# All four weight pairs of the first half issued by ScalarE

## The chip, the cores and the metric

The kernel runs on one core of one Trainium2 chip. The metric is the device time of one execution, in microseconds. Of the 40 runs of the kernel before, 39 lie within 0.2% of their median of 486.8 us (all from 486.38 to 488.38), and the effect told here is only a few times that, so kernels are compared by several runs taken in alternation with the kernel before on the same chip. A "ratio" in this document is the mean time of one kernel's fast runs over the mean of the other's fast runs of the same rounds, so it is not quite the ratio of the medians that stand beside it.

## The reference

Two attention blocks share an input x of 2048 rows by 1024 columns (bf16): block A is linear attention, block B a dilated sliding window. A gate mixes their outputs. The first thing that either needs is x times a weight matrix; the kernel begins with block B's v.

```python
qkv = x @ wqkv            # x: 2048 x 1024, wqkv: 1024 x 3072, for block A and for block B
...                       # attention of each block, then @ wo
g = sigmoid((x * gate_w).sum(-1, keepdims=True))
return g * a + (1 - g) * b
```

## The kernel before

The kernel is a list of operations with dependencies and priorities, which a small scheduler of its own puts in order for each engine before the program is built. Only the head of the program matters here. The x tile of rows 128t to 128t+127 is loaded by a DMA transpose and called x0, x1, ... below. The weights of v come in two halves of 512 columns; each half is loaded as four "pairs", each of two 128-row chunks, 256 KB.

```python
def load_x(t, prio):
    e_, r = t // 8, t % 8
    return P.op("sp", lambda e: e.dma_start_transpose(xT[:, :, t * 128:(t + 1) * 128], x2[e_, r * 128:(r + 1) * 128, :]),
                1.5, writes=[xT.part((0, 8), (t * 128, (t + 1) * 128))], prio=prio, chan="x%d" % t, lat=1.3)

def load_w(slot, half, src, c0, prio, d0=0, d1=8, eng="sp", after=()):
    n = d1 - d0
    return P.op(eng, lambda e: e.dma_start(ws[slot][:, d0:d1, half * 512:half * 512 + 512], src[:, d0:d1, c0:c0 + 512]), ...)

load_x(0, 0)                                       # x0, SyncE
load_w(0, 0, Bw, 2048, 0.1, 0, 2, "act")           # half one, pair 1, ScalarE
load_w(0, 0, Bw, 2048, 0.2, 2, 4, "act")           # pair 2, ScalarE
load_w(0, 0, Bw, 2048, 0.3, 4, 6)                  # pair 3, SyncE
load_w(0, 0, Bw, 2048, 0.4, 6, 8)                  # pair 4, SyncE
for t in range(1, NT):
    load_x(t, 3 + t)                               # x1 ... x15, SyncE
for d in range(0, 8, 2):
    load_w(0, 1, Bw, 2560, 6.1 + 0.1 * d, d, d + 2)   # half two, four pairs, SyncE
# ... cut: warm-up matmuls on a zeroed tile ...
for t, half in [(4 * b + i, half) for b in range(NT // 4) for half in range(2) for i in range(4)]:
    # ... cut ...
    step = 2 if t == 0 else 8
    for d in range(0, 8, step):                    # x0: two matmuls as each pair lands; others: eight at once
        o = group(bank, xs, w, [xr, ws[0].part((d, d + step), (half * 512, half * 512 + 512))], d, d + step)
    # ... cut: eviction to vst by ScalarE or VectorE, then a store by SyncE ...
```

The matmul engine thus runs x0 with pairs 1 to 4 (eight matmuls, two for each pair), then x1, x2, x3 with half one (24), then x0 to x3 with half two, and so on.

## Time and profile before

| | before |
|---|---|
| time, median of the first 3 runs | 486.82 us (486.45 to 486.95) |
| profiled span | 485.2 us |
| matmul engine busy | 474.2 us, 98% |
| first real matmul | 5.54 us |
| matmuls without another wait for a load from | 15.30 us |

From the page of the kernel before: the span, the busy line (PE is the matmul engine, PEld its weight loads, then VectorE, ScalarE, GpSimd; x counts instructions), and the first line of the chain that ended last.

```profile
span 485.2 us, 10105 instructions
...
PE 474.2 (98%) x4339; PEld 222.8 (46%) x4403; DVE 285.2 (59%) x547; ACT 140.2 (29%) x227; POOL 5.9 (1%) x36
...
PE 95%; SPq 2%; issue 1%; DMA 1%; ACT 0%; DVE 0%
```

The matmul engine, busy for 98% of the span and with 95% of the chain that ended last, is the limit almost from end to end. What is left to win is where it waits. The timeline of the head shows that. Columns are start and duration in us, engine (SPq and ACTq are SyncE's and ScalarE's issue of DMAs), line, operation, count, and in brackets the idle time before the piece and what ended it.

```profile
0.80 1.38 SPq L1308 DMA_TRANSPOSE xT<-in_A_x_dram  x1
0.80 0.94 ACTq L1313 DMA_DIRECT2D w<-in_B_wqkv_dram  x2
...
2.24 1.06 SPq L1313 DMA_DIRECT2D w<-in_B_wqkv_dram  x2
...
3.35 4.92 SPq L1308 DMA_TRANSPOSE xT<-in_A_x_dram  x3
...
5.54 1.47 PE L1334 MATMUL ps_all<-w,xT 128*128 128x512 bf16 x6 [0.28 <-DMA xT<-in_A_x_dram]
...
7.25 0.60 PE L1334 MATMUL ps_all<-w,xT 128*128 128x512 bf16 x2 [0.24 <-DMA w<-in_B_wqkv_dram]
...
8.17 6.82 PE L1334 MATMUL ps_all<-w,xT 128*128 128x512 bf16 x30 [0.32 <-DMA xT<-in_A_x_dram]
8.31 2.12 SPq L1313 DMA_DIRECT2D w<-in_B_wqkv_dram  x4
...
15.30 17.00 PE L1334 MATMUL ps_all<-w,xT 128*128 128x512 bf16 x77 [0.30 <-DMA w<-in_B_wqkv_dram]
```

Read it from the fifth line down. The first matmuls start at 5.54, when x0 is there. The last two of x0's eight start at 7.25, when pair 4 is there. The x1 group starts at 8.17, and at 15.30 the last pair of half two ends the last wait. Six, two and thirty matmuls make 38 before 15.30.

The table of stretches of the same kernel gives the DMA rate. The columns used are the stretch, its length, then the busy times, and at the end of the row the granted matmul clock (1.00 is full speed), the DMA share and GB/s. The DMA share is the time that DMA packets took, over sixteen engines; it passes 1 here (1.28 at 6.5 to 7.5 us).

```profile
core 0: us, PE busy (x) PEld busy (x) DVE busy (x) ACT busy (x) POOL busy (x), PEclk, DMA share, GB/s
2.50:5.50 3.00, 2.76 (x9) 0.92 (x7) 1.29 (x10) 0.56 (x1) 2.58 (x14) 1.00 1.08 302
...
6.50:7.50 1.00, 0.76 (x5) 0.13 (x3) 0.19 (x1) 0.00 (x0) 0.00 (x0) 1.00 1.28 267
7.50:8.50 1.00, 0.69 (x4) 0.21 (x3) 0.00 (x0) 0.60 (x1) 0.00 (x0) 1.00 1.14 239
8.50:9.50 1.00, 1.00 (x7) 0.41 (x5) 0.00 (x0) 0.00 (x0) 0.00 (x0) 1.00 1.06 243
9.50:10.50 1.00, 1.00 (x6) 0.47 (x5) 0.00 (x0) 0.39 (x1) 0.00 (x0) 1.00 0.56 110
10.50:11.50 1.00, 1.00 (x7) 0.47 (x5) 0.00 (x0) 0.21 (x1) 0.00 (x0) 1.00 1.06 322
```

A stretch with transposes alone (7.5 to 9.5) moves about 240 GB/s; the stretch from 2.5 to 5.5, for most of which x0 from SyncE ran beside pairs 1 and 2 from ScalarE, moved 302. At 9.5 to 10.5, where SyncE's queue turns from transposes to pairs, there is a slack spot.

One more reading: when each load landed. The trace records sixteen completions for each load. The matmuls that wait for a load start just after its sixteenth (pair 4's at 7.25 us, after 7.21; x1's at 8.17, after 8.13). "Landed" below is the sixteenth, and "spread" is the time from the first to the sixteenth. Before, pair 3 landed at 6.36 us, pair 4 at 7.21 (spread 0.20), x1 at 8.13, x2 at 9.14, x3 at 10.20.

### The profile page before, as it was taken

To read this page: it belongs to the slowest core of one execution; us is meant where nothing else is said; L and a number is where in the kernel's file an instruction comes from. 1 tells how busy PE (TensorE), PEld (TensorE's weight loads), DVE (VectorE), ACT (ScalarE), POOL (GpSimd) and SP (SyncE) were. 2 spreads that over 40 slices of the span, in tenths; PEclk is the share of its full clock that TensorE was granted. 3 is DMA by queue.
4 is the path that set the end of the run, shared out by engine and by line. 5 is a ranking of instruction groups with operands and counts; after the bars stand their busy time and mean duration, and the time that the engine had idled before them with its cause. 6 is when DMAs were issued, how large, how long until landed. Compare 5 with 4: busy or idle time off the path is not lost.

```text
span 485.2 us, 10105 instructions
## 1 busy us (share of the span) xinstructions
PE 474.2 (98%) x4339; PEld 222.8 (46%) x4403; DVE 285.2 (59%) x547; ACT 140.2 (29%) x227; POOL 5.9 (1%) x36
## 2 busy tenths in 40 slices
PE   8999999999999999999999999999999999999997
PEld 3444444444444444454544554444444444444443
DVE  2121435888688888665666556496579236653434
ACT  2111121235322234334443333455532230111000
POOL 4000000000000000000000000000000000000000
PEclk9999999999999999999999999999999999999999
DMA  8999993132014459433222322820086018830212
GB/s 224 222 194 299 309 355 122 65 110 86 1 44 135 107 138 245 100 76 86 55 75 67 85 66 66 204 54 2 10 217 163 1 15 242 221 24 2 88 68 89
DMA packets 72951, 57.39 MB, mean 118 GB/s; under 512 B 37953, under 2 KB 60865, under 8 KB 72898
## 3 DMA queue, kind: packets, MB, share of 16 engines
q1 hardware_dynamic: 72210, 56.07, 44.3%
q8 instruction: 36, 0.59, 0.5%
q10 hardware_dynamic: 688, 0.59, 0.4%
q14 instruction: 17, 0.14, 0.1%
HBM read 34.49 MB, written 13.76 MB: 99 GB/s over the span
## 4 chain that ended last, share of the span: by engine, by line
PE 95%; SPq 2%; issue 1%; DMA 1%; ACT 0%; DVE 0%
PE ps_all L1334 78%; PE ps_all L1693 11%; PE ps_all L1463 2%; PE ps_all L1440 2%; SPq L1308 1%; DMA w<-in_B_wqkv_dram 1%; PE ps_all L1556 1%; SPq L1313 1%; PE ps_all L1638 0%; PE ps_all L1610 0%; ACT e L1341 0%; DVE o L1697 0%
## 5 line engine op out<-in xcount | busy, mean ns | idle before, releaser
L1334 PE MATMUL ps_all<-w,xT 128*128 128x512 bf16 x924 | 208.6, 379 | 4.5 <-issue 2.1
L1334 PE MATMUL ps_all<-xT,w 128*128 128x512 bf16 x745 | 166.3, 379 | 2.2 <-issue 1.4
L1334 PEld LDWEIGHTS ps_all<-w,xT 128*128 128x128 bf16 x960 | 91.2, 98 | 111.1 <-DMA w<-in_B_wqkv_dram 2.1
L1334 PEld LDWEIGHTS ps_all<-xT,w 128*128 128x128 bf16 x768 | 73.9, 98 | 88.7 <-issue 1.3
L1693 PE MATMUL ps_all<-w,qT 128*128 128x512 bf16 (+1 forms) x260 | 55.4, 372 | 0.2
L1693 PEld LDWEIGHTS ps_all<-w,qT 128*128 128x128 bf16 x264 | 25.9, 98 | 29.6
L1365 DVE CAST vst<-ps_all 128x512 bf16<-128x512 f32 x15 | 10.4, 694 | 43.5 <-PE ps_all L1334 43.5
L1448 ACT ACTIVATE E<-ps_all 128x1824 bf16<-128x1824 f32 (+1 forms) x18 | 30.4, 1689 | 13.4 <-PE ps_all L1440 13.4
L1345 DVE TENSOR_SCALAR e<-e 128x512 bf16<-128x512 bf16 x64 | 18.4, 290 | 26.9 <-ACT e L1343 14.0
L1697 DVE SCALAR_TENSOR_TENSOR o<-ps_all,gm,xT 128x512 bf16<-128x512 f32 (+1 forms) x25 | 18.0, 728 | 21.1 <-PE ps_all L1693 20.8
L1341 ACT ACTIVATE e<-ps_all 128x512 bf16<-128x512 f32 x32 | 19.1, 598 | 39.0 <-PE ps_all L1334 38.1
L1343 ACT ACTIVATE e<-ps_all 128x512 bf16<-128x512 f32 x32 | 19.1, 598 | 32.3 <-PE ps_all L1334 32.3
L1295 DVE TENSOR_TENSOR mx<-mx,kT 128x1024 bf16<-128x1024 bf16 x32 | 20.9, 688 | 10.9 <-ACT kT L1366 10.8
L1295 DVE TENSOR_TENSOR mx<-mx,qT 128x1024 bf16<-128x1024 bf16 x32 | 20.8, 687 | 7.9 <-ACT qT L1369 7.9
L1451 DVE TENSOR_TENSOR E<-E,msk 128x1824 bf16<-128x1824 bf16 (+1 forms) x18 | 19.9, 1104 | 7.8 <-ACT E L1448 7.4
L1366 ACT ACTIVATE vst<-ps_all 128x512 bf16<-128x512 f32 x17 | 10.2, 601 | 48.5 <-PE ps_all L1334 45.1
L1480 DVE TENSOR_TENSOR ot<-ps_all,rs 128x512 bf16<-128x512 f32 x36 | 23.3, 686 | 0.0
L1366 ACT ACTIVATE az<-ps_all 128x512 bf16<-128x512 f32 x22 | 13.2, 601 | 34.5 <-PE ps_all L1334 34.5
L1366 ACT ACTIVATE kT<-ps_all 128x512 bf16<-128x512 f32 x20 | 11.9, 597 | 37.6 <-PE ps_all L1334 37.6
L1347 DVE SCALAR_TENSOR_TENSOR pk<-ps_all,e 128x512 bf16<-128x512 f32 x32 | 22.0, 689 | 0.7
L1369 ACT ACTIVATE qT<-ps_all 128x512 bf16<-128x512 f32 x19 | 11.4, 598 | 37.4 <-PE ps_all L1334 37.3
L1369 ACT ACTIVATE xT<-ps_all,g 128x512 bf16<-128x512 f32 x10 | 6.9, 689 | 45.1 <-PE ps_all L1334 45.1
(72 smaller groups left out, 260.2 us busy)
## 6 DMA issues: line engine op xcount, KB each, us to landing
rb<-rc_hbm SPq DMA_DIRECT2D x32, 256.0 KB, 5.2
w<-in_A_wqkv_dram SPq DMA_DIRECT2D x6, 1024.0 KB, 9.0
v<-vB_hbm SPq DMA_DIRECT2D x36, 132.0 KB, 2.7
vB_hbm<-vst SPq DMA_DIRECT2D x32, 132.0 KB, 6.2
w<-in_B_wqkv_dram SPq DMA_DIRECT2D x4, 1024.0 KB, 9.5
xn<-in_A_x_dram SPq DMA_DIRECT2D x16, 256.0 KB, 2.7
out_dram<-o SPq DMA_DIRECT2D x15, 256.0 KB, 2.1
oB_hbm<-ot SPq DMA_DIRECT2D x36, 96.0 KB, 2.2
```

The lines of the kernel that those rows point to most:

```text
L1295: P.op("dve", lambda e, m=m, op=op: e.tensor_tensor(m[:, 0:n], m[:, 0:n], src, op), 0.08 + n / 1920.0, reads=[m.all(), reg], writes=[m.all()],
L1334: last = e.matmul(bank.ap(), lhs(dc), rhs(dc), start=(dc == 0), stop=(dc == 7))
L1341: P.op("act", lambda e: e.activation(e_[:, :], bank.ap(), ACT.Exp), act(512), reads=[bank.iv], writes=[e_.all()])
L1343: P.op("act", lambda e: e.activation(e_[:, :], bank.ap(), ACT.Exp, accum_out=qe[:, col:col + 1]), act(512) + 0.1, reads=[bank.iv], writes= ...
L1345: P.op("dve", lambda e: e.tensor_scalar(e_[:, :], e_[:, :], 1.0, 1e-6, op0=ALU.min, op1=ALU.add), 0.25, reads=[e_.all()], writes=[e_.all()])
L1347: P.op("dve", lambda e: e.scalar_tensor_tensor(out=dst, in0=bank.ap(), scalar=0.0, in1=e_[:, :], op0=ALU.max, op1=ALU.add), dps(512), read ...
L1366: fa = lambda e: e.activation(dst, src(), ACT.Copy)
L1369: fa = lambda e: e.activation(dst, src(), ACT.Copy, scale=scale)
L1448: P.op("act", lambda e: e.activation(E[:, 0:32 * nq].rearrange("p (j q) -> p j q", j=4), ps[:, 4:8, 0:8 * nq], ACT.Exp), act(32 * nq), rea ...
L1451: P.op("dve", lambda e: e.tensor_tensor(ev(), ev(), m[:, :, :].rearrange("p r q -> p (r q)")[:, None, :].to_broadcast([128, 16, 2 * nq]), ...
L1480: P.op("dve", lambda e, r=r, bv=bv, h=h: e.tensor_tensor(o[:, 512 * h:512 * h + 512].rearrange("p (k i c) -> p k i c", k=2, c=32), bv()[:, ...
L1693: last = e.matmul(bank.ap(0, f1 - f0), qT[:, dc, t * 128:(t + 1) * 128], ws[3][:, dc, f0:f1], start=(dc == 0), stop=(dc == 7))
```

## The change

The intent: SyncE's queue should carry only transposes until half two, so that x1, x2 and x3 start earlier and half two follows sooner; ScalarE, which between its issues and its first eviction at 7.90 us has only a table load of 1.28 us, takes all four pairs.

```diff
         load_w(0, 0, Bw, 2048, 0.1, 0, 2, "act")
         load_w(0, 0, Bw, 2048, 0.2, 2, 4, "act")
-        load_w(0, 0, Bw, 2048, 0.3, 4, 6)
-        load_w(0, 0, Bw, 2048, 0.4, 6, 8)
+        load_w(0, 0, Bw, 2048, 0.3, 4, 6, "act")
+        load_w(0, 0, Bw, 2048, 0.4, 6, 8, "act")
```

The order of the matmul engine's instructions does not change. A few evictions move from ScalarE to VectorE, and x4 and x5 are issued ahead of the first store of vst.

## The prediction

> What bounds the kernel now. The matrix engine does: the page's first part has PE busy 474.2 of 485.2 us (98%), and the chain that ended last is 95% PE. From 15.30 us to the end the chain is an almost unbroken run of matmuls, and the waits from 16 to 100 us name no DMA before a matmul. A change of load order can therefore win only what PE loses before 15.30 us.
>
> What is lost there. The timeline shows the first real matmul at 5.54 us, released by the first transposed tile x0 (issued at 0.80, 4.7 us to landing). Between 5.54 and 15.30 us PE runs 6+2+30 = 38 matmuls. In the steady run 49 take 10.74 us, 0.219 us each by that line and about 0.216 us by start-to-start, so 38 need 8.2 us and take 9.76: about 1.5 us are waits. They are on the weight pairs of half one (to 7.25), on the second tile x1 (8.17 us) and on the last pairs of half two (15.06 to 15.30). That 1.5 us, 0.3% of the span, is a ceiling.
>
> What the change does. SyncE now issues x0, pair 3, pair 4 (0.56 and 0.46 us of issue), x1, x2, x3, four half-two pairs. After it: x0, x1, x2, x3, half-two pairs. x1 should start issuing near 2.24 instead of 3.35 us. ScalarE issues four pairs, ending near 2.7 instead of 1.74; its 1.28 us table load moves about 0.95 us later, to 4.0, still far ahead of its first eviction at 7.90: free. PE's instruction order is unchanged; a few evictions and copies swap between ScalarE and VectorE, and x4 and x5 go ahead of the first vst store. VectorE is 59% busy, ScalarE 29%: free too.
>
> Why issue time does not become gain one for one. The 16 DMA engines are busy from 2.5 us on: 315 GB/s while x0 and two pairs run from two queues, 247 GB/s when transposes run alone (7.2 to 9.5), 322 GB/s for pairs alone (10.5 to 13.5). [...] the two-queue stretch agrees, being no faster than one queue of pairs. So bytes needed before the second group (x0, four pairs, x1) stay the same; only pairs 3 and 4 now share with x1 rather than going ahead of it. Whichever lands later decides. Also x2 took 2.27 us to issue instead of 1.25, so SyncE is sometimes held back by what is outstanding; x2 and x3 will not move a full microsecond.
>
> What should be won: the switch from transposes to copies inside one queue has a slack spot (110 GB/s at 9.5 to 10.5; a smaller one near 5 us). The early one goes away, and transposes mix with copies longer. I estimate x1 and pair 4 both there by 7.7 to 7.8 us, 0.3 to 0.5 us sooner, and the half-two pairs 0.3 to 1.0 us sooner, with the wait at 15.1 us mostly gone. Net gain about 0.6 us, between nothing and 1.4.
>
> Prediction: 486.2 us, range 485.4 to 487.0. Faster by over 2%: 0.005; within 2%: 0.99; slower by over 2%: 0.005.
>
> What would show it. Right: first real matmul still at 5.5; the x1 group at 7.6 to 7.9; the long unbroken run starting by 14.8; the rest unchanged in length; PE still 98%. Wrong: pair 3 or 4 landing later than 6.4 and 7.2 us and holding the first group longer; x0 itself later; half-two pairs no earlier because SyncE's transposes back up; new waits for x4 onwards; or a different ScalarE/VectorE split making PE wait for banks between 60 and 130 us.

## The result, and the profile after

| | before | after |
|---|---|---|
| time, median of 6 runs | 486.84 us (486.42 to 487.34) | 489.57 us (488.80 to 491.35) |
| ratio after / before | | 1.0063, 95% interval 1.0041 to 1.0085 |
| profiled span | 485.2 us | 487.5 us |

The change made the kernel slower by 0.6%: far below 2%, but clear of noise, and outside the predicted range of 485.4 to 487.0. The same parts of the page of the kernel after:

```profile
span 487.5 us, 10102 instructions
...
PE 474.8 (97%) x4339; PEld 223.3 (46%) x4403; DVE 289.8 (59%) x555; ACT 134.9 (28%) x219; POOL 5.8 (1%) x36
...
PE 96%; DMA 2%; issue 1%; ACTq 0%; ACT 0%; DVE 0%
```

The busy time of the matmul engine grew by 0.6 us, so about 1.7 of the 2.3 us of the span are idle time. The 0.6 lies in the eleven warm-up matmuls before the first real one, which took 4.84 us instead of 4.01. The timeline of the head shows where the idle time is:

```profile
0.80 9.50 SPq L1308 DMA_TRANSPOSE xT<-in_A_x_dram  x4
0.80 2.14 ACTq L1313 DMA_DIRECT2D w<-in_B_wqkv_dram  x4
...
5.92 1.03 PE L1334 MATMUL ps_all<-w,xT 128*128 128x512 bf16 x4
...
7.72 0.60 PE L1334 MATMUL ps_all<-w,xT 128*128 128x512 bf16 x2 [0.76 <-DMA w<-in_B_wqkv_dram]
10.34 2.12 SPq L1313 DMA_DIRECT2D w<-in_B_wqkv_dram  x4
...
10.59 23.70 PE L1334 MATMUL ps_all<-w,xT 128*128 128x512 bf16 x107 [2.27 <-DMA w<-in_B_wqkv_dram]
```

The matmuls of pairs 1 and 2 start at 5.92, and those of pair 3 at 7.72 (before, at 5.54 and 6.41). Then the engine waits until 10.59, and the line names the load of a weight: it is pair 4, which landed at 10.54 us instead of 7.21, although ScalarE had issued it by 2.94 us. After 10.59 there is no further wait for a load. Put both kernels on one scale: after, six matmuls had started before the run from 10.59; the 39th, at about 0.219 us each (49 take 10.74 us in the steady run), comes at 10.59 + 32 x 0.219 = 17.6 us. Before, it started at 15.30. The difference, 2.3 us, is that of the spans, as near as these figures tell.

The first line shows the other half of the story: SyncE needed 9.50 us to issue four transposes, and half two was issued at 10.34 instead of 8.31 us. The table of stretches of the kernel after:

```profile
core 0: us, PE busy (x) PEld busy (x) DVE busy (x) ACT busy (x) POOL busy (x), PEclk, DMA share, GB/s
2.50:5.50 3.00, 3.00 (x9) 1.06 (x7) 1.29 (x10) 1.28 (x1) 2.58 (x14) 1.00 1.05 282
...
6.50:7.50 1.00, 0.45 (x3) 0.00 (x0) 0.19 (x1) 0.00 (x0) 0.00 (x0) 1.00 1.18 144
7.50:8.50 1.00, 0.60 (x2) 0.11 (x2) 0.00 (x0) 0.00 (x0) 0.00 (x0) 1.00 1.23 172
8.50:9.50 1.00, 0.00 (x0) 0.00 (x0) 0.00 (x0) 0.00 (x0) 0.00 (x0) 1.00 1.30 168
9.50:10.50 1.00, 0.00 (x0) 0.00 (x0) 0.00 (x0) 0.00 (x0) 0.00 (x0) 1.00 1.23 100
```

From 6.5 to 10.5 us the DMA engines are marked busy (a share above 1) but move only 100 to 172 GB/s. Before, the same stretches had 267, 239 and 243, then the slack spot. That is what had to be explained: two queues that shared the engines at 282 GB/s while x0 and the first pairs ran, and at about half of it when x1 met pairs 3 and 4.

### The profile page after: what moved, and what is told of

Its sections match the earlier page's. It is cut to its first block, busy times and chain, and to the rows that moved or that the text cites. A ratio compares the mean times of both kernels' runs of the same rounds, so it can differ in the third digit from the quotient of the medians.

```text
span 487.5 us, 10102 instructions
## 1 busy us (share of the span) xinstructions
PE 474.8 (97%) x4339; PEld 223.3 (46%) x4403; DVE 289.8 (59%) x555; ACT 134.9 (28%) x219; POOL 5.8 (1%) x36
## 4 chain that ended last, share of the span: by engine, by line
PE 96%; DMA 2%; issue 1%; ACTq 0%; ACT 0%; DVE 0%
PE ps_all L1334 79%; PE ps_all L1693 11%; PE ps_all L1463 2%; PE ps_all L1440 2%; DMA w<-in_B_wqkv_dram 2%; PE ps_all L1556 1%; PE ps_all L1638 0%; PE ps_all L1610 0%; ACTq L1313 0%; ACT e L1341 0%; DVE o L1697 0%
## 5 line engine op out<-in xcount | busy, mean ns | idle before, releaser
L1366 ACT ACTIVATE kT<-ps_all 128x512 bf16<-128x512 f32 x18 | 10.7, 597 | 39.2 <-PE ps_all L1334 39.2
L1430 DVE TENSOR_SCALAR qd<-qT,par 128x912 bf16<-128x912 bf16 (+1 forms) x34 | 14.6, 452 | 9.3 <-PE ps_all L1440 9.3
L1369 ACT ACTIVATE qT<-ps_all 128x512 bf16<-128x512 f32 x15 | 9.0, 597 | 39.4 <-PE ps_all L1334 39.4
```

Of the source, the lines that this page charges most:

```text
L1366: fa = lambda e: e.activation(dst, src(), ACT.Copy)
```

## The experiments

The theory at the outset: a transpose from one queue that overlaps copies from the other slows both. The rivals: plain sharing of the engines by packets of two sizes; unlucky HBM addresses; SyncE's back-pressure; ScalarE's queue being served worse; and the position in ScalarE's queue.

### e1_pair4_sync: only pair 3 moves

```diff
-        load_w(0, 0, Bw, 2048, 0.4, 6, 8, "act")
+        load_w(0, 0, Bw, 2048, 0.4, 6, 8)
```

> Edit: pair 4 goes back to SyncE ahead of x1; pairs 1 to 3 stay on ScalarE. Theory ([...] transposes from one queue and copies from another slow both): only pair 3 can overlap transposes of x1 and pair 4 is out of it; pair 4 lands by 7.3 us, the unbroken run of matmuls starts by 8.4 us on the group of x1, time 486.3 to 487.3. Rival (the last pair is late only because it is fourth in ScalarE's queue): now pair 3 is the last there; pair 3 would land late instead, after 8 us, and the time be near 488.

Measured: 486.90 us median against 487.06 of the kernel before, ratio 1.0003 (0.9987 to 1.0020). Pair 3 landed at 7.19, pair 4 at 7.40, x1 at 8.20 us. The timeline of its matmuls:

```profile
5.94 1.04 PE L1334 MATMUL ps_all<-w,xT 128*128 128x512 bf16 x4 [0.38 <-DMA xT<-in_A_x_dram]
...
7.23 11.12 PE L1334 MATMUL ps_all<-w,xT 128*128 128x512 bf16 x49 [0.26 <-DMA w<-in_B_wqkv_dram]
```

From 7.23 us on no wait is long enough for the timeline to part it. One moved pair costs nothing; the whole loss comes with the second, which is the one that meets x1. Pair 3 is now the last of ScalarE's queue and lands before pair 4, which speaks against the position in the queue.

### e2_plain_x: x1 to x3 not transposed (wrong result)

```diff
+            if t in (1, 2, 3):
+                return P.op("sp", lambda e: e.dma_start(xT[:, :, t * 128:(t + 1) * 128], x2[e_, r * 128:(r + 1) * 128, :].rearrange("p (c s) -> p c s", s=128)),
+                            1.5, ... )        # same rows, same place, same 256-byte pieces, no transpose
```

> Wrong result on purpose. Edit on the changed kernel: x1, x2 and x3 are plain copies of the same rows to the same place in 256-byte pieces, issued by SyncE in the same place; nothing is transposed but x0 and x4 on. Theory [...]: no collapse, 280 GB/s or more between 5.5 and 8 us, pair 4 lands by 7.8 us, time 485.5 to 487. Rivals that need no transpose (turns between small and large packets of two queues, or two streams meeting at the same HBM addresses): the rate stays under 200 GB/s, pair 4 lands at 9.5 us or later, time 488.5 to 490.

Measured: 488.06 us median, ratio 1.0027 (1.0011 to 1.0044). Pair 4 landed at 8.96 us (spread 0.78), x1 at 9.19. The stretches (length, busy times, clock, DMA share, GB/s as before):

```profile
6.50:7.50 1.00, 1.00 (x6) 0.33 (x4) 0.19 (x1) 0.00 (x0) 0.00 (x0) 1.00 1.20 265
7.50:8.50 1.00, 0.22 (x2) 0.00 (x0) 0.00 (x0) 0.00 (x0) 0.00 (x0) 1.00 1.21 285
8.50:9.50 1.00, 0.50 (x3) 0.26 (x4) 0.00 (x0) 0.00 (x0) 0.00 (x0) 1.00 1.35 225
```

Neither side was right. The rate does not collapse, so the fall to 144 GB/s needs the transposes. But pair 4 is still 1.75 us later than in the kernel before, so plain sharing does a good part of the harm.

### e4_x1_after_pair2: x1 held until pair 2 has landed

```diff
-        load_w(0, 0, Bw, 2048, 0.2, 2, 4, "act")
+        held = load_w(0, 0, Bw, 2048, 0.2, 2, 4, "act")
         for t in range(1, NT):
-            load_x(t, 3 + t)
+            load_x(t, 3 + t, after=[held])
```

Half two waits for the same landing; the gate weights, the second copies of x and the first two stores of vst are held back too, so that nothing else slips ahead. The same is so in e5, e7 and e9.

> Edit on the changed kernel: SyncE waits for the landing of pair 2 (near 5.4 us) before it issues x1; all four pairs stay on ScalarE. Theory: pairs 3 and 4 run alone and land near 6.3 and 7.1 us; x1 then lands near 8.5 to 9.0; no stretch under 200 GB/s; time 486.5 to 488.0, clearly under the changed kernel's 489.6. Rival (four pairs on ScalarE are slow whatever SyncE does): pair 4 still lands at 9 us or later, time 489 or more.

Measured: 488.49 us median, ratio 1.0047 (1.0025 to 1.0069). Pair 3 landed at 6.40, pair 4 at 7.92 (its first completion at 6.89), x1 at 9.25 us. Pair 4 came 2.6 us sooner than in the changed kernel with the same four pairs in ScalarE's queue, so the number of pairs there is not the cause. The rate, though, was 139 GB/s from 6.5 to 7.5, against the expectation: as I read it, x1's first rows (issued from 5.14 us) met the tail of pair 4. And the price of the delay, x1 at 9.25, eats most of the gain. One of the four runs took 490.30 us at a mean clock of 0.997, the others 488.10 to 488.78 at 1.0.

### e5_x2_after_pair4: only x1 beside the pairs

```diff
-        load_w(0, 0, Bw, 2048, 0.4, 6, 8, "act")
+        held = load_w(0, 0, Bw, 2048, 0.4, 6, 8, "act")
         for t in range(1, NT):
-            load_x(t, 3 + t)
+            load_x(t, 3 + t, after=[held] if t >= 2 else ())
```

> Edit on the changed kernel: x1 is issued right behind x0 as there, but x2, x3 and half two wait for the landing of pair 4. Theory: the transpose of x1 alone is enough; pairs 3 and 4 meet it, the rate collapses again (under 220 GB/s from 6 us on), though for fewer bytes: pair 4 lands between 8 and 10 us; the time is no better than 488.5 because x2 starts late. Rival (SyncE's back-pressure on x2 and x3, each 3.3 us in issue, is what holds ScalarE's pairs): with neither of them outstanding pair 4 lands by 7.6 us.

Measured: 491.21 us median, ratio 1.0094 (1.0077 to 1.0111). Pair 4's completions came from 7.43 to 9.10 us, x1 landed at 9.28. The stretches:

```profile
6.50:7.50 1.00, 0.64 (x3) 0.11 (x2) 0.19 (x1) 0.00 (x0) 0.00 (x0) 1.00 1.17 253
7.50:8.50 1.00, 0.00 (x0) 0.00 (x0) 0.00 (x0) 0.00 (x0) 0.00 (x0) 1.00 0.22 48
8.50:9.10 0.60, 0.00 (x0) 0.00 (x0) 0.00 (x0) 0.00 (x0) 0.00 (x0) 1.00 0.00 0
```

Back-pressure falls: x2 and x3 were not even issued, and pair 4 still lands at 9.10. The rows show a new thing. Up to 7.5 us the rate is fair (253 GB/s, against the expectation of under 220), then the engines are nearly idle (DMA share 0.22, then 0.00) while the last completions of pair 4 and of x1 are still missing. So a small part of pair 4 was far behind the rest: fifteen of its sixteen completions had come by 8.39 us, the last came at 9.10. The trace does not name the DMA engine of a packet, so whether one engine was late can't be said. The four runs took 489.91 us at a mean clock of 1.0, 490.78 and 491.76 at 0.996, and 491.65 at 1.0, so here too something besides the clock varies.

### e6_other_weights: pairs 3 and 4 from another tensor (wrong result)

```diff
-        load_w(0, 0, Bw, 2048, 0.3, 4, 6, "act")
-        load_w(0, 0, Bw, 2048, 0.4, 6, 8, "act")
+        load_w(0, 0, Aw, 2048, 0.3, 4, 6, "act")
+        load_w(0, 0, Aw, 2048, 0.4, 6, 8, "act")
```

> Wrong result on purpose. Edit on the changed kernel: pairs 3 and 4 are read from the other weight tensor, so from another place in HBM. Theory: nothing changes, pair 4 lands between 9.5 and 11 us, time 488.7 to 490.5. Rival (the two streams meet at unlucky HBM addresses): pair 4 lands by 8.5 us, time under 488.

Measured: 489.31 us median, ratio 1.0063 (1.0047 to 1.0079), the ratio of the change itself. Pair 4 landed at 10.36 us. The place in HBM is not the cause. (One of the four runs took 490.91 us at a mean clock of 0.997.)

### e7_x1_after_pair4: no overlap at all beyond x0

The edit is that of e4 with the wait on pair 4.

> Edit on the changed kernel: x1 waits for the landing of pair 4, so that no transpose but x0 meets a pair, at the price of an idle stretch of DMA. Theory: pair 4 lands near 7.1 us with its 16 completions within 0.5 us; x1 lands near 10.2 us; the matmul engine waits about 2.5 us for it, as long as in the changed kernel, and the median is near the changed kernel's, 488.5 to 489.5. Second point, the changed kernel's two runs at 491 us with a mean granted clock of 0.996: if a wait of some 2 us at this place is what lets the clock drop in some runs, then one to three of the runs here show it as well, 1.5 to 2.5 us slower than the others with a mean clock of 0.995 to 0.998; if it belongs to the overlap, none does.

Measured: 490.32 us median, ratio 1.0083 (1.0069 to 1.0097). Pair 3 landed at 6.20 us (spread 0.08), pair 4 at 7.05 (0.20), x1 at 10.61. The matmuls:

```profile
5.67 2.03 PE L1334 MATMUL ps_all<-w,xT 128*128 128x512 bf16 x8
...
10.65 6.33 PE L1334 MATMUL ps_all<-w,xT 128*128 128x512 bf16 x28 [2.96 <-DMA xT<-in_A_x_dram]
```

All eight matmuls of x0 go through from 5.67, then 2.96 us pass until x1. This is the clean figure for ScalarE issuing all four pairs: 7.05 us, even a little sooner than before the change. What delays pair 4 is the company, not the issuer. The time is worse than expected because x1 landed 0.4 us later than I had put it. One of the five runs had a mean clock of 0.996; it took 491.47 us. Another took 491.14 at a clock of 1.0, so the clock is not the only thing that varies here.

### e9_plain_x1_only: the fourth cell of a table (wrong result)

The edit is e5 with x1 loaded as in e2.

> Wrong result on purpose. Edit on e5_x2_after_pair4: x1, the only tile beside pairs 3 and 4 there, is a plain copy in 256-byte pieces. With e2, e5 and the changed kernel this fills a table of two by two for the landing of pair 4 (alone 7.05 us in e7): plain x1 to x3 8.96, transposed x1 9.10, transposed x1 to x3 10.54. Theory (two parts that add: the other queue's bytes are served in turn, and a transpose beside copies costs more than its bytes): pair 4 between 7.5 and 8.1 us, its 16 completions within 0.6 us, where e5 had 9.10 and 1.67. Rival (the transpose adds nothing, the difference was luck): pair 4 at 8.8 us or later.

Measured: 489.68 us median, ratio 1.0057 (1.0040 to 1.0074). Pair 4 landed at 8.46 us (spread 0.60). That lies between theory and rival. The table, with the landing of pair 4 in us and the spread of its completions in brackets, one profile each:

| beside pairs 3 and 4 | plain copies | transposes |
|---|---|---|
| nothing (e7) | 7.05 (0.20) | 7.05 (0.20) |
| x1 alone (e9, e5) | 8.46 (0.60) | 9.10 (1.67) |
| x1, x2, x3 (e2, the change) | 8.96 (0.78) | 10.54 (2.51) |

So of the 3.5 us between the first and the last cell, 1.9 come with plain copies of the same bytes, and 1.6 come on top when they are transposes. That both parts are there is shown, but not their exact sizes: the other profiles of the changed kernel's head have pair 4 at 10.49 (e11) and 9.99 (e12). In the plain column a part of the delay is already in pair 2 and x0, which landed at 5.81 and 6.00 us in e9 and at 5.15 and 5.45 in e5; why they were later with a plain x1 is not shown.

### e10_swap_issuers: ScalarE transposes, SyncE copies

```diff
-            return P.op("sp", lambda e: e.dma_start_transpose(...
+            return P.op("act" if t < 4 else "sp", lambda e: e.dma_start_transpose(...
-        load_w(0, 0, Bw, 2048, 0.1, 0, 2, "act")     # and pairs 2 to 4
+        load_w(0, 0, Bw, 2048, 0.1, 0, 2)            # and pairs 2 to 4
```

> Edit on the changed kernel: issuers swapped, ScalarE issues the transposes of x0 to x3 and SyncE the four pairs; half two and x4 wait for x3, so the time is not to be compared, only the landing of pair 4. Theory (it is the overlap, not whose queue): pair 4 lands at 9.5 us or later. Rival (ScalarE's queue is served worse than SyncE's): pair 4 by 8 us, the transposes late in its place.

Measured: pair 4 landed at 10.17 us, with the transposes in ScalarE's queue and the pairs in SyncE's. It is the overlap, whichever queue holds which. (Its time, 492.63 us, is one run and holds later waits of its own.)

This profile also caught something that the others did not. Its stretches, cut where its clock records change; the third number from the end is the granted clock:

```profile
6.55:9.96 3.41, 1.32 (x6) 0.21 (x3) 0.14 (x1) 0.00 (x0) 0.00 (x0) 1.00 1.13 170
9.97:13.37 3.40, 3.15 (x8) 1.19 (x9) 0.00 (x0) 1.88 (x2) 0.00 (x0) 0.50 0.65 155
13.38:16.00 2.62, 2.62 (x14) 1.18 (x12) 0.70 (x1) 0.14 (x1) 0.00 (x0) 1.00 0.46 138
```

For 3.41 us, from 9.96 us and so just before the matmuls resumed at 10.22, the matmul clock was granted at one half: 8 matmuls took 3.15 us there, 0.39 each, and 14 took 2.62, 0.19 each, in the stretch after. In the stretch before it the matmul engine was busy for only 1.32 of 3.41 us. Whether that brought the drop on, one profile does not show. Half speed for 3.41 us of matmuls costs half of it, about 1.7 us by estimate from these rows.

### e3_all_sync: all four pairs on SyncE, nothing in two queues

```diff
-        load_w(0, 0, Bw, 2048, 0.1, 0, 2, "act")     # and pairs 2 to 4
+        load_w(0, 0, Bw, 2048, 0.1, 0, 2)            # and pairs 2 to 4
```

> Edit on the changed kernel, the opposite way: all four pairs go to SyncE, between x0 and x1, so nothing overlaps in two queues. (The first store of vst is held behind half two, so that the order stays that of the kernel before.) Theory (the loss is the overlap of a transpose with copies of the other queue): no completion spread over 1 us among the pairs of half one; pair 4 by 7.7 us, x1 by 8.7 us, time 486.6 to 487.8, so clearly under the changed kernel. Rival (ScalarE's share of the issue is worth a microsecond in itself): 488 or more.

Measured: 488.21 us median, ratio 1.0032 (1.0016 to 1.0047). The matmuls:

```profile
6.05 2.00 PE L1334 MATMUL ps_all<-w,xT 128*128 128x512 bf16 x6
...
8.26 0.60 PE L1334 MATMUL ps_all<-w,xT 128*128 128x512 bf16 x2 [0.22 <-DMA w<-in_B_wqkv_dram]
...
9.24 6.65 PE L1334 MATMUL ps_all<-w,xT 128*128 128x512 bf16 x30 [0.37 <-DMA xT<-in_A_x_dram]
```

This missed the expectation of 486.6 to 487.8, and it is a point against the first form of the theory. x0 landed at 4.33 us, early, but pair 1 only at 6.00 with a spread of 1.03 us, just over what I had allowed, although no other queue was active. So some completions lag on copies that follow a transpose in the same queue as well, here by about a microsecond. With an overlap the lag was larger (2.51 us for pair 4 in the changed kernel) and the other queue ran ahead (160 KB of x2 had been moved there by 10.5 us); it is not the only thing that can start one. It also shows that letting ScalarE issue pairs 1 and 2 is worth about a microsecond: in the kernel before, where it does, x1 lands at 8.13, here at 9.19.

### e8_half2_scalar: the same cost in another place

On the kernel before, half one unchanged:

```diff
-        for t in range(1, NT):
+        for t in range(1, 4):
             load_x(t, 3 + t)
         for d in range(0, 8, 2):
-            load_w(0, 1, Bw, 2560, 6.1 + 0.1 * d, d, d + 2)
+            half2 = load_w(0, 1, Bw, 2560, 6.1 + 0.1 * d, d, d + 2, "act", after=[held])   # held: pair 3
+        for t in range(4, NT):
+            load_x(t, 3 + t, after=[half2])
```

> Edit on the kernel before: half one stays as there, but the four pairs of half two go to ScalarE, released by the landing of pair 3, so that they meet the transposes of x1, x2 and x3; x4 and on wait for half two. A second place for the same suspected cost. Theory: the rate falls under 220 GB/s while they overlap (8 to 11 us) where the kernel before has 247, x3 lands after 11.5 us instead of 10.2, half two later than 15 us, time 487.8 to 490. Rival (only the head of the program, with pairs 3 and 4, is special): 280 GB/s or more, x3 by 11 us, half two by 13 us, time 487 or less.

Measured: 488.81 us median, ratio 1.0041 (1.0025 to 1.0056). x3 landed at 13.61 instead of 10.20 us, and half two at 14.26 (15.02 in the kernel before). The matmuls:

```profile
8.19 3.72 PE L1336 MATMUL ps_all<-w,xT 128*128 128x512 bf16 x16 [0.20 <-DMA xT<-in_A_x_dram]
...
13.66 4.71 PE L1336 MATMUL ps_all<-w,xT 128*128 128x512 bf16 x21 [1.74 <-DMA xT<-in_A_x_dram]
```

The engine stands 1.74 us for a transposed tile. Pairs on ScalarE's queue beside transposes on SyncE's cost time here too, this time to the transposes. The expectation was right on the time and on x3, and wrong on half two and mostly on the rate: that was 351 GB/s at 8.5 to 9.5, where the packet records hold copies alone (x2's rows had all been moved before, x3's had not begun), then 242 and 214 in the next two microseconds, where x3 runs beside the pairs. x3 took from 9.5 to 13.6 us for what takes about one microsecond in the kernel before (x2 landed at 9.14, x3 at 10.20). Part of this loss is thus simply that the pairs were served beside it and before it.

### e11_after_again: the changed kernel once more

> The changed kernel itself again, as a control. Pair 4 lands between 9.8 and 11 us in the profile; ratio to the kernel before 1.005 to 1.007. Of its 5 or 6 runs one to three show a mean granted clock under 0.998 and are 1.5 to 2.5 us slower than the rest; the rest lie at 488.5 to 489.6.

Measured: 490.93 us median, ratio 1.0085 (1.0070 to 1.0100). Pair 4 landed at 10.49 us. One run took 489.62 at a mean clock of 0.999; the four others took 490.91 to 491.41 at 0.996 or 0.997. That was more of them than expected, and the ratio lies above the expected 1.005 to 1.007.

### e12_keep_busy: ten matmuls in the wait

```diff
                 o = group(bank, xs, w, ...)
+                if (t, half, d) == (0, 0, 4):                    # after the two matmuls of pair 3
+                    for i in range(10):
+                        P.op("pe", lambda e: e.matmul(banks[7].ap(), warm[:, 0:128], warm[:, :], start=True, stop=True), 0.22, ..., after=[o])
```

> Edit on the changed kernel: ten matmuls on the zeroed warm-up tile, into a bank that nothing reads, between the pair-3 and the pair-4 matmuls of the first group, so that the matmul engine is busy for about 2.2 us of its wait for pair 4. They do nothing for the transfers. Theory (two costs: the late pair 4, near 2.4 us in every run, and in some runs a granted clock of one half for 3.41 us, near 1.9 us more, that the idle stretch brings on): pair 4 lands at 10 to 11 us as before, no run has a mean clock under 0.998, all runs lie within 488.6 to 489.9. Rival (the slower runs have another cause): two or more of the runs stay at 490.5 or more.

Measured: 489.40 us median (489.03 to 489.89), ratio 1.0052 (1.0038 to 1.0066), mean clock 1.0 in all five runs. The matmuls:

```profile
6.15 1.52 PE L1334 MATMUL ps_all<-w,xT 128*128 128x512 bf16 x6 [0.61 <-DMA xT<-in_A_x_dram]
...
7.51 2.32 PE L1388 MATMUL ps_all<-warm 128*128 128x512 bf16 x10
...
10.04 8.16 PE L1334 MATMUL ps_all<-w,xT 128*128 128x512 bf16 x37 [0.21 <-DMA w<-in_B_wqkv_dram]
```

The ten idle matmuls fill the wait and end before pair 4 (9.99 us). The transfers are as late as before, but no run is of the slower kind any more: none of five, where the changed kernel has six of its eleven runs (in e11 and in the result) at 0.996 or 0.997. That is as the theory has it, but with so few runs not proof: if the extra matmuls did nothing, five of these sixteen runs drawn at random would still hold no slow one about once in 17 times (an estimate from the counts), and e12 ran on another chip than e11.

## Why the prediction was wrong

What held. The matmul engine bounds the kernel, its order and its busy time did not change, and nothing after the head moved: the difference of the 39th matmul is the difference of the spans. The later table load on ScalarE and the swap of evictions cost nothing that the profile shows. The prediction's own list of what would make it wrong named both things that came: pairs 3 and 4 landing later and holding the first group, and half two no earlier because SyncE's transposes back up (9.50 us for the issue of four, half two issued at 10.34 instead of 8.31).

What failed is this step: "I estimate x1 and pair 4 both there by 7.7 to 7.8 us". They landed at 10.75 and 10.54 us. Three things were wrong in or behind it.

1. "So bytes needed before the second group (x0, four pairs, x1) stay the same". SyncE's queue does not stop at x1. Before the change pair 4 stood ahead of x1 and so ahead of everything behind it. After it, x1 and x2 run beside it: the packets of SyncE's queue between 5.5 and 10.5 us moved 422 KB, which is x1 (262 KB) and 160 KB of x2. A queue's order was a priority, and the change gave it away. With plain copies in place of the transposes this part alone puts pair 4 at 8.96 us instead of 7.05.
2. The rate. I took the good rate of x0 beside pairs 1 and 2 (315 GB/s in the prediction, 302 in the longer stretch shown before) for the rate of x1 beside pairs 3 and 4. It was 144 to 172, then 100. With plain copies it stays at 225 to 285 (e2), with another HBM place it does not recover (e6, pair 4 at 10.36 us), and with the issuers swapped pair 4 is as late (e10, 10.17). So it belongs to transposes that overlap copies, and it puts pair 4 about 1.0 to 1.6 us further back. The two-queue stretch was no faster than one queue of pairs (315 GB/s against 322), and I read that as "no slower either".
3. The clock was left out. After the wait of 2.3 us for pair 4, right after one of 0.76, some runs have a lower mean granted clock: six of eleven are at 0.996 or 0.997, where none of the 34 runs of the kernel before that have a clock on record is under 0.999. The changed kernel's five runs at a clock of 0.999 or 1.0 average 489.29 us, its six others 491.16. So it loses about 2.4 us to the late pair in every run, and 1.9 us more in the runs with the lower clock. e10's profile shows one such drop, of about 1.7 us by the estimate there, and in e12, with the engine kept busy and the transfers as they were, no slower run was seen. That the wait brings the drop on is thus likely, not proven; it does not do so every time, and e5 and e7 each have one of the longer runs at a clock of 1.0.

What stays open: why some completions come late when copies meet or follow a transpose, as in e5 (fifteen of pair 4's by 8.39 us, the last at 9.10) and e3 (pair 1's over 1.03 us), and why x0 beside pairs 1 and 2 was spared: 265 to 322 GB/s at 2.5 to 5.5 us in the eleven profiles read where ScalarE issues these pairs. Whether the transposes beside it wait for the late part can be read in part. The completions of pair 4 in the changed kernel are spread over 2.51 us, while the sixteen of x1 all come from 10.45 to 10.75, with the last of pair 4's; with plain x1 they spread over 1.21 us (e2). The packet records of the same trace add this: sixteen 256-byte packets of SyncE's queue that started from 9.63 to 9.78 us all ended from 10.39 to 10.42, just as pair 4's last seven completions came (10.38 to 10.54). The median 256-byte packet there takes 0.018 us. So the transposes' packets waited and were let go together. What they waited for the trace does not show; that it was the late part of pair 4 is argued from the times alone.

The same thing is in the kernel before, where one queue alone is active. There half two's pairs stand ahead of a store and of x4 in SyncE's queue, yet the last two pairs' completions spread over 1.77 and 1.72 us. From 14.0 to 15.0 us the rate falls to 147 and then 50 GB/s, and 22 packets of 256 bytes that started from 13.79 to 14.93 all end from 15.26 to 15.30, after the last pair landed at 15.02. The last wait for a load in that kernel, to 15.30, falls in this stretch. So a second queue is one way to get transposes and unfinished copies under way together, not the only one.

No version of these beats the kernel before by more than the noise. e1, with three pairs on ScalarE, is level with it.

## What to carry to other kernels

The order within one DMA queue was a priority here (pair 4 landed at 7.21 us ahead of x1 in SyncE's queue, at 10.54 beside it): moving a load to a second queue let what had stood behind it run beside it (x1 and 160 KB of x2), so cost such a move with the bytes of the whole other queue and not only with the issue time saved. Keep DMA transposes from overlapping copies that the critical path waits for (pair 4 at 10.54 us with the overlap, at 7.05 without it in e7). Putting those copies ahead of them in the same queue did it for pairs 3 and 4 here (spread 0.20 us), but not for the last pairs of half two (1.77 and 1.72), so look at the spread of completions and not only at the order of issue. Check a shared rate in the very mix that the change will make. A stall of the matmul engine of two to three microseconds may cost its clock as well (0.996 or 0.997 in six of eleven runs here, 1.9 us longer): look at the mean granted clock of every run, not only at the profiled one.
